# Two cached attention blocks on one core: the maximum over partitions moved from GpSimd to TensorE and VectorE, and the identity made without the library's select

## The chip, the cores and the metric

The kernel runs on one core of a Trainium2 chip. The time is the device time in microseconds of one execution, the median of several. In the profile PE is the matrix engine (TensorE), PEld its weight loads, DVE the vector engine, ACT the scalar engine, POOL GpSimd, SP the engine that issues most DMAs. Lines such as L338 are lines of the kernel file.

## The reference

Two blocks A and B of one decoding step each, side by side in the output. Both have 4 batches, 32 query heads, 8 key/value heads, head size 128, a cache of 8192 tokens; B looks only at the last 2048.

```python
q = (x @ wq).reshape(B, 1, 32, 128).transpose(0, 2, 1, 3)
k, v = repeat(k_cache, 4, axis=1), repeat(v_cache, 4, axis=1)   # B: last 2048 tokens
scores = einsum("bhqd,bhkd->bhqk", q, k) * 128 ** -0.5
o = einsum("bhqk,bhkd->bhqd", softmax(scores), v)
out = o.transpose(0, 2, 1, 3).reshape(B, 1, 4096) @ wo          # A and B concatenated
```

All inputs are bf16. The caches that are read, with the weights, are 184.6 MB.

## The kernel before

The work is cut into 20 units: four of block B (one batch with all 8 heads each), then sixteen of block A (one batch and two heads each). A unit has 4 MB of K and 4 MB of V, loaded into two slots each (`kv_load`). The 128 partitions of a slot hold different tokens, so a softmax runs over 128 partitions and 128 places in each. For block A the rows of 32 KB go to the partitions in the order 32 x 4, so that a partition's head follows from its number modulo 4; the masks `MASKA` and `MASKB` put -1e30 on the scores of the head that a partition does not hold.

Per unit `u`, in PE's order: K is transposed on PE in 16 groups of four f32 transposes (`pe_T`, L283) and copied out of PSUM by DVE and ACT in turn (L299); the scores are 16 groups of matmuls three groups behind (`pe_S`, L322), the first half into bank `SA[u % 2]`, the second into `SB`; near the end come the sums of the exponentials of the unit before (`pe_SM`, L350, into the other `SA`); and, after the last scores, the 128 matmuls of the unit before with its V (`pe_PV`, L338), in eight chunks of 16.

Meanwhile the maximum of unit `u` is taken: DVE reduces the two halves along the free dimension (`dve_max`, L420), adds the mask (`dve_addmask`, `M1m`), GpSimd reduces over the partitions and puts the result on all of them (`pool_ar1`, L441, `MB`), DVE takes the mask off (`dve_submask`, `MBm`), subtracts from both halves of the scores (`dve_sub`, L458), and ACT makes the exponentials (`act_exp`, L469). DVE takes the sum of the exponentials of the unit before (`dve_sum`, L476) between the masked maximum and `dve_submask`, and after the subtractions normalises the unit before (`add_norm`), whose end is `otr`.

Every two units (a turn of a hardware loop on PE; `turn`) one piece of the output projection runs beside the rest (`pe_job_OT`, `pe_job_OL`, `pe_job_OPJ`) and is added to `oacc` by DVE (L404, `ocp`).

Order comes from the order of each engine's list (`plan`) and from semaphores. SP issues the loads in one list: both Wq, K of units 0 and 1, then K(u), V(u-1) for each u, a piece of Wo for every second unit. V(u) waits for `otr(u-2)`, K(u) of block A for `otr(u-3)` (early ones for the transposes of u-2), the pieces of Wo for `ocp`; an entry that waits holds all behind it. V of the last unit comes in three chunks (`VL`), the last piece of Wo in eight (`WL`).

At the start GpSimd fills the buffers (`pool_setup0`, `pset`), makes the bf16 and f32 identities `ident` and `identf` by `affine_select` (`pool_setup1`, `setup`), the permutation `permE`, and from `EO`, which DVE reduces out of `ident`, the masks. The queries are made on PE (`pe_job_xT`, `pe_job_QP`, `pe_job_perm`), first for B, then for A; Wq lies in the V slots until then, so V(0) waits for B's queries. GpSimd copies each unit's queries to `RQc` (`pool_rq`).

The tail, after the loop: half of the last value product (chunks 0 to 3, with the first part of V), `pe_SM` of the last unit, `pe_seed` (L679: `oacc` put into two PSUM banks by f32 matmuls), the other four chunks, `add_norm`, 16 matmuls with the last piece of Wo (L700) on top of the seed, two copies and two stores.

Of the kernel before, what the change touches and what calls it, by code (L numbers as in the profile page):

```python
# [14 lines left out]
def bass_concat_heads__gqa_block_cached__sliding_block_cached__decode_kernel(  # L15
# [12 lines left out]
):  # L28
    ReduceOp = bass.bass_isa.ReduceOp

# [8 lines left out]
    NSEG = 4  # L39
# [33 lines left out]
    with ExitStack() as es:  # L73
# [8 lines left out]
        def sm(name):  # L82
# [16 lines left out]
        M1m = sb("M1m", [128, NSEG * C], F32)  # L99
        MB = sb("MB", [128, NSEG * C], F32)  # L100
        MBm = sb("MBm", [128, NSEG * C], F32)
# [11 lines left out]
        OTp = sb("OTp", [128, C, Bn], BF16)  # L113
        ORx = sb("ORx", [C * Bn, C, C, 128 // C], BF16)
        MSK = sb("MSK", [C * Bn, C], BF16)
        SEL = sb("SEL", [C * Bn, Bn], BF16)
        EO = [sb("EO%d" % P, [128, 2], F32) for P in range(2)]
        OL = sb("OL", [128, C, Bn], BF16)
# [9 lines left out]
                 "out0", "out1", "out2", "Tq", "Td", "Ta", "S", "PV", "Ed", "Ea", "Eq", "vs", "sub", "exp", "otr", "otp",  # L128
                 "ocp", "Ef", "fin0", "fin1", "ar1", "SM", "msk", "pset", "setup", "pm0", "pm1", "oc", "ocB", "mkb", "perm", "rq"]
        sems = {n: sm("s_" + n) for n in names}  # L130
# [103 lines left out]
        def pe_job_perm(P):  # L234
            idx = perm_idx[P] = new_job("perm", "act")
            bk = kbank(idx)

            def fn(pe):
                ins = None
                for e in range(2):  # L240
                    ins = pe.matmul(out=bk[:, e * Bn * HQ:(e + 1) * Bn * HQ],
                                    lhsT=permE[:, e, :, :].rearrange("p t i -> p (t i)"),
                                    rhs=QT[:, P, :, :].rearrange("p b h -> p (b h)"), start=True, stop=True)
                return ins
            op("pe", fn, waits=[("E", qp_idx[(P, NQP - 1)]), ("perm",), bankfree(idx)], inc=("T", idx))

            def efn(act):
                ins = None
                for tl in range(2):
                    ins = act.activation(  # L250
                        out=RQ[P][64 * tl:64 * tl + 64, :, :, :, C * tl:C * tl + C].rearrange("p b g e c -> p e (b g) c"),
                        in_=bk[64 * tl:64 * tl + 64, 0:2 * Bn * HQ].rearrange("p (e s c) -> p e s c", e=2, c=C), func=ACTF.Copy)
                return ins
            add(dict(eng="act", fn=efn, waits=[("T", idx)], inc=("E", idx)))

# [47 lines left out]
        def pool_rq(u):  # L303
            un = units[u]
            w = [("E", perm_idx[un["P"]])]
            if un["P"] == 1:
                src = RQ[1][:, un["b"], :, :, :]
            else:
                src = RQ[0][:, un["b"], un["gp"]:un["gp"] + 1, :, :].broadcast_to([128, NSEG, 2, 2 * C])
            return dict(eng="pool", fn=lambda pool: pool.tensor_copy(out=RQc[:, u % 2, :, :, :], in_=src), waits=w, inc=("rq", u))  # L310
# [16 lines left out]
        def pe_PV(u, c, bank=None, waits=()):  # L327
# [3 lines left out]
            def fn(pe):  # L331
# [8 lines left out]
                return ins  # L340
            op("pe", fn, waits=waits, inc=("PV", u * NC + c))

# [93 lines left out]

        def pool_ar1(u):
            n = ncol(u)

            def fn(pool):  # L440
                return pool.partition_all_reduce(MB[:, 0:n], M1m[:, 0:n], channels=128, reduce_op=ReduceOp.max)  # L441
            return dict(eng="pool", fn=fn, waits=[("pm", u, 0)], inc=("ar1", u))

        def dve_submask(u):
            n, P = ncol(u), units[u]["P"]

            def fn(dve):
                return dve.tensor_tensor(out=MBm[:, 0:n], in0=MB[:, 0:n], in1=MASK[P][:, 0:n], op=AluOpType.subtract)
            return dict(eng="dve", fn=fn, waits=[("ar1", u)], inc=("pm", u, 1))
# [71 lines left out]

        def pool_setup0(pool):
            pool.memset(dummy[:, :], 0.0)
            pool.memset(onesf[:, :], 1.0)
            pool.memset(onesb[:, :], 1.0)
            pool.memset(RQ[0][:, :, :, :, :], 0.0)
            pool.memset(RQ[1][:, :, :, :, :], 0.0)
            pool.memset(OT_sb[:, :, :, :, :], 0.0)
            pool.memset(oacc[:, :], 0.0)
            pool.memset(PT[:, :, :], 0.0)  # L530
            return pool.memset(Wo_sb[:, :, :], 0.0)
        op("pool", pool_setup0, inc=("pset",))

        def pool_setup1(pool):
            ins = pool.affine_select(out=ident[:, :], in_=onesb[:, :], pattern=[[1, 128]],
                                     compare_op=AluOpType.is_equal, fill=0.0, base=0, channel_multiplier=-1)
            ins = pool.affine_select(out=identf[:, :], in_=onesf[:, :], pattern=[[1, 128]],  # L537
                                     compare_op=AluOpType.is_equal, fill=0.0, base=0, channel_multiplier=-1)
            return ins
        op("pool", pool_setup1, waits=[("pset",)], inc=("setup",))  # L540

# [7 lines left out]
        def dve_msk(dve):  # L549
            idv = ident[0:NR, 0:NR].rearrange("p (h b) -> p h b", h=C)  # L550
            dve.tensor_reduce(out=EO[1][:, :], in_=ident[:, :].rearrange("p (i s) -> p s i", s=2), axis=AX.X, op=AluOpType.max)
            dve.tensor_reduce(out=EO[0][:, :], in_=ident[:, :].rearrange("p (i s m) -> p s i m", s=2, m=2), axis=AX.XY, op=AluOpType.max)
            dve.tensor_reduce(out=MSK[:, :], in_=idv, axis=AX.X, op=AluOpType.max)
            return dve.tensor_reduce(out=SEL[:, :], in_=idv.rearrange("p h b -> p b h"), axis=AX.X, op=AluOpType.max)
        op("dve", dve_msk, waits=[("setup",)], inc=("msk",))
        def pool_mask2(pool):
            for P, g in ((0, 1), (1, NSEG)):
                ins = pool.tensor_scalar(out=MASK[P][:, :].rearrange("p (g s h) -> p g s h", g=g, s=2),
                                         in0=EO[P][:, :].rearrange("p (g s h) -> p g s h", g=1, h=1).broadcast_to([128, g, 2, REP]),
                                         scalar1=-1.0, scalar2=BIG, op0=AluOpType.add, op1=AluOpType.mult)  # L560
            return ins
        op("pool", pool_mask2, waits=[("msk",)], inc=("mkb",))

        def dma(dst, src):
# [10 lines left out]
        for P in (1, 0):  # L575
# [3 lines left out]
            pe_job_perm(P)  # L579
        op("pe", None, waits=[("E", perm_idx[0]), ("setup",), ("msk",)])  # L580
        op("dve", None, waits=[("msk",)])
        add(pool_rq(0))
# [13 lines left out]
        while pc < NC:  # L596
            TOK.append(("PV", pc))
            pc += 1
        assert pc == NC
        AFTER = {("S", 2): ("OT",), ("S", 5): ("OL",)}  # L600

        for u in range(NU):
# [8 lines left out]
            for tok in TOK:  # L611
# [11 lines left out]
                elif tok[0] == "SM":  # L623
                    pe_SM(u - 1)
                else:
                    pe_PV(u - 1, tok[1], waits=[("V", u - 1) if u >= 1 else None] if tok[1] == 0 else [])
# [6 lines left out]
            for k in range(0, NJ, 2):  # L633
# [3 lines left out]
                for d in extra.get(k, []):  # L637
                    add(d)
            add(dve_max(u, 1))
            if units[u]["P"] == 0:  # L640
                add(dve_maxc(u))
            add(dve_addmask(u))
            if u >= 1:
                add(dve_sum(u - 1))
                add(dve_rcp(u - 1))
            add(dve_submask(u))
            add(dve_sub(u, 0))
# [18 lines left out]
            if u + 1 < NU:  # L666
                add(pool_rq(u + 1))
            add(pool_ar1(u))
            if u >= 1 and units[u - 1]["P"] == 0:
# [12 lines left out]
        add(dve_rcp(L))  # L682
        VCH = [4, 3, 1]
        vch_of = [i for i, n in enumerate(VCH) for _ in range(n)]
        for c in range(NC):
# [3 lines left out]
            if c == 4:  # L689
                pe_SM(L)  # L690
                op("pe", pe_seed, waits=[("ocp", NTURN - 1)])
            pe_PV(L, c, bank=KTB[0], waits=w)
# [15 lines left out]
        def kv_load(kind, u):  # L708
# [21 lines left out]
            if kind == "V" and u == L:  # L730
                c0 = 0
                for i, n in enumerate(VCH):
                    t0, t1 = c0 * TC, (c0 + n) * TC
                    src = bass.AP(tensor=base.tensor, offset=base.offset + t0 * DH, ap=[[NT * DH, 32], [32 * NT * DH, 4], [1, (t1 - t0) * DH]])
                    op("sp", dma(buf[:, slot, t0:t1, :].rearrange("p t d -> p (t d)"), src), waits=w, inc=("VL", i))
                    c0 += n
                return
            src = bass.AP(tensor=base.tensor, offset=base.offset, ap=[[NT * DH, 32], [32 * NT * DH, 4], [1, NT * DH]])
            sem = sem_of((kind, u))
            bump = 16 * (NPART[kind] - 1)  # L740
            op("sp", lambda sp: sp.sem_inc(sem, bump), waits=w, bump=(sem, bump, None))
            if kind == "K" and u == L:
                for h in range(2):
                    t0 = h * NTH
                    src = bass.AP(tensor=base.tensor, offset=base.offset + t0 * DH, ap=[[NT * DH, 32], [32 * NT * DH, 4], [1, NTH * DH]])
                    op("sp", dma(buf[:, slot, t0:t0 + NTH, :].rearrange("p t d -> p (t d)"), src), inc=(kind, u, 0) if h == 0 else ("KH", u))
# [189 lines left out]
```

## Time and profile before

| what | us |
|---|---|
| median of 5 runs | 439.43 (439.05 to 439.77) |
| the profiled execution, its own time | 439.61 |
| its span, first to last instruction | 437.6 |
| PE busy | 364.3 (83%) |
| DVE busy | 209.9 (48%) |
| ACT busy | 194.9 (45%) |
| POOL busy | 27.6 (6%) |
| POOL partition_all_reduce (L441), 20 times | 7.7 |
| first PE instruction (L201) | 20.61 |
| first K transpose (L283) | 34.00 |
| HBM read | 184.56 MB, 422 GB/s over the span |

How to read a profile line: start and length in microseconds, engine, line, operation, what it writes `<-` what it reads with partitions x elements, how many; in square brackets the idle time of the engine before it and what ended it. In the lines of the stage view the columns are the window, its length, the busy time of PE, PEld, DVE, ACT and POOL with the number of instructions, the granted clock of PE as a share of full speed, the busy share of the DMA engines, and GB/s. In the page's slices each digit is the busy share of a fortieth of the span in tenths. A PE that is busy is not a PE at its peak, since matmuls are pipelined.

### The profile page before, as it was taken

What the parts mean: (1) busy time and instruction counts of PE and PEld (TensorE: products, weight loads), DVE (VectorE), ACT (ScalarE), POOL (GpSimd) and SP (SyncE); (2) the same over time, 40 slices, a digit from 0 to 9 for tenths busy, and PEclk for the clock granted to TensorE, in tenths of its full rate; (3) what the DMA queues carried; (4) which work ended last, traced back from release to release, by engine and by line L of the source; (5) the groups of instructions that cost most, each with busy time, mean ns of one, the idle gap of its engine ahead of it and who ended that gap; (6) DMA issues with size and microseconds to landing.
All of it is one profiled execution on the core that took longest, in us unless ns stands there. A gap on an engine that the chain in (4) does not pass through costs nothing.

```text
span 437.6 us, 15525 instructions
## 1 busy us (share of the span) xinstructions
PE 364.3 (83%) x7174; PEld 337.3 (77%) x7184; DVE 209.9 (48%) x406; ACT 194.9 (45%) x249; POOL 27.6 (6%) x88
## 2 busy tenths in 40 slices
PE   0068998998998959896989598969878895989996
PEld 0068897997996959795979588868868795979975
DVE  0004555664564634463456247525644563456651
ACT  1024474473663625271635254434535361537540
POOL 6100000000000000000000000000100000000000
PEclk9999999999999997999999899989998999799999
DMA  8999999999999999999999999999999999999996
GB/s 336 433 428 412 427 415 428 420 443 407 449 431 434 422 435 431 434 425 434 431 431 428 431 431 428 435 429 431 419 443 431 431 429 431 431 431 419 437 421 237
DMA packets 10996, 184.73 MB, mean 422 GB/s; under 512 B 1236, under 2 KB 2280, under 8 KB 2408
## 3 DMA queue, kind: packets, MB, share of 16 engines
q1 hardware_dynamic: 10960, 184.56, 99.0%
q8 instruction: 8, 0.13, 0.1%
q10 hardware_dynamic: 24, 0.01, 0.0%
q14 instruction: 4, 0.03, 0.0%
HBM read 184.56 MB, written 0.01 MB: 422 GB/s over the span
## 4 chain that ended last, share of the span: by engine, by line
PE 54%; DMA 41%; issue 2%; DVE 1%; SPq 1%; ACT 1%
DMA K_sb<-in_A_k_cache_dram 29%; PE KT L283 26%; PE OT L338 11%; DMA K_sb<-in_B_k_cache_dram 7%; PE SB L322 5%; PE SA L322 4%; DMA V_sb<-in_A_v_cache_dram 4%; PE KT L396 4%; PE SA L350 1%; PE KT L338 1%; SPq L566 1%; DVE oacc L404 1%; PE KT L263 1%; ACT KT_sb L299 1%; DVE OS L501 0%
## 5 line engine op out<-in xcount | busy, mean ns | idle before, releaser
L283 PE MATMUL KT<-identf,K_sb 128*128 128x128 f32 x1280 | 206.8, 295 | 44.6 <-DMA K_sb<-in_A_k_cache_dram 32.3
L299 ACT ACTIVATE KT_sb<-KT 128x1024 bf16<-128x1024 bf16 (+1 forms) x192 | 165.0, 881 | 120.0 <-PE KT L283 120.0
L283 PEld LDWEIGHTS KT<-identf,K_sb 128*128 128x128 f32 x1280 | 146.8, 149 | 49.8 <-DMA K_sb<-in_A_k_cache_dram 33.2
L299 DVE COPY KT_sb<-KT 128x512 int32<-128x512 int32 x160 | 110.4, 690 | 131.9 <-PE KT L283 130.5
L338 PE MATMUL OT<-PT,V_sb 128*128 128x64 bf16 x2560 | 78.1, 193 | 1.0 <-issue 0.6
L338 PEld LDWEIGHTS OT<-PT,V_sb 128*128 128x128 bf16 x2560 | 75.9, 98 | 1.2 <-issue 0.7
L469 ACT ACTIVATE PT<-Dt 128x512 bf16<-128x512 f32 x40 | 24.6, 630 | 84.0 <-DVE Dt L458 84.0
L322 PEld LDWEIGHTS SA<-RQc,KT_sb 128*128 128x128 bf16 x1280 | 57.0, 98 | 2.3
L322 PEld LDWEIGHTS SB<-RQc,KT_sb 128*128 128x128 bf16 x1280 | 51.1, 97 | 7.9 <-issue 4.4
L322 PE MATMUL SA<-RQc,KT_sb 128*128 128x16 bf16 x1280 | 56.4, 170 | 0.0
L322 PE MATMUL SB<-RQc,KT_sb 128*128 128x16 bf16 x1280 | 52.9, 170 | 0.0
L420 DVE TENSOR_REDUCE M<-SB 128x8 f32<-128x512 f32 (+1 forms) x20 | 13.8, 692 | 50.1 <-PE SB L322 50.1
L441 POOL PARTITION_ALL_REDUCE MB<-M1m x20 | 7.7, 385 | 334.3 <-DVE M1m L434 334.3
L396 PE MATMUL KT<-Wo_sb,OL 128*4 128x512 bf16 x80 | 18.9, 379 | 0.0
L201 PE MATMUL KT<-ident,x_sb 4*128 4x4 bf16 x8 | 0.6, 170 | 20.6 <-POOL identf L537 20.6
L201 PEld LDWEIGHTS KT<-ident,x_sb 4*128 4x128 bf16 x8 | 0.4, 114 | 20.8 <-issue 20.8
L476 DVE TENSOR_REDUCE LB<-SA 128x8 f32<-128x512 f32 (+1 forms) x20 | 13.7, 684 | 2.8 <-PE SA L350 2.8
L458 DVE TENSOR_TENSOR Dt<-SA,MBm 128x512 f32<-128x512 f32 x20 | 13.8, 691 | 0.7
L367 DVE TENSOR_TENSOR ORx<-KT,MSK 32x1024 bf16<-32x1024 bf16 x10 | 12.1, 1212 | 3.5 <-PE KT L362 3.5
L458 DVE TENSOR_TENSOR Dt<-SB,MBm 128x512 f32<-128x512 f32 x20 | 13.6, 681 | 0.0
L420 DVE TENSOR_REDUCE M<-SA 128x8 f32<-128x512 f32 (+1 forms) x20 | 13.6, 681 | 0.0
L350 PE MATMUL SA<-PT,onesb 128*128 128x128 bf16 x168 | 12.7, 218 | 0.0
(69 smaller groups left out, 118.1 us busy)
## 6 DMA issues: line engine op xcount, KB each, us to landing
K_sb<-in_A_k_cache_dram SPq DMA_DIRECT2D x15, 4096.0 KB, 23.1
V_sb<-in_A_v_cache_dram SPq DMA_DIRECT2D x15, 4096.0 KB, 30.2
K_sb<-in_B_k_cache_dram SPq DMA_DIRECT2D x8, 2048.0 KB, 23.8
V_sb<-in_B_v_cache_dram SPq DMA_DIRECT2D x16, 1024.0 KB, 18.7
V_sb<-in_B_wq_dram SPq DMA_DIRECT2D x1, 4096.0 KB, 12.3
V_sb<-in_A_wq_dram SPq DMA_DIRECT2D x1, 4096.0 KB, 21.5
Wo_sb<-in_B_wo_dram SPq DMA_DIRECT2D x4, 1024.0 KB, 12.0
K_sb<-in_A_k_cache_dram SPq DMA_DIRECT2D x2, 2048.0 KB, 17.5
```

The lines of the kernel that those rows point to most:

```text
L283: ins = pe.transpose(out=bkf[:, pi * 128:(pi + 1) * 128], in_=K_sbf[:, slot, t0:t0 + 2, :].rearrange("p t d -> p (t d)"), identity=identf[ ...
L299: ins = e.tensor_copy(out=d, in_=r) if eng == "dve" else e.activation(out=d, in_=r, func=ACTF.Copy)
L322: ins = pe.matmul(out=stb[:, t % NTH * C:(t % NTH + 2) * C], lhsT=ktv[:, pi, :, e], rhs=RQc[:, u % 2, t // TS, e, :], start=(e == 0), stop ...
L338: ins = pe.matmul(out=otb[:, s * NW:s * NW + w], lhsT=V_sb[:, slot, t, :], rhs=PT[:, slot, t * C:t * C + w], start=(j == 0), stop=(j == n ...
L350: ins = pe.matmul(out=SA[u % 2][:, s * NM:(s + 1) * NM], lhsT=onesb[:, :], rhs=PT[:, u % 2, c0:c0 + NM], start=(i == 0), stop=(i == n - 1))
L367: return dve.tensor_tensor(out=ORx[:, :, :, :], in0=bk[0:NR, 0:128].rearrange("p (i o r) -> p r o i", o=1, r=C).broadcast_to([NR, C, C, 12 ...
L396: ins = pe.matmul(out=bk[0:Bn, 0:D], lhsT=OL[:, i, :], rhs=Wo_sb[:, i, :], start=(i == 0), stop=(i == C - 1))
L420: return dve.tensor_reduce(out=M1[:, h * n:(h + 1) * n].rearrange("p (s h) -> p s h", h=C), in_=bank[:, :].rearrange("p (s j h) -> p s h j ...
L441: return pool.partition_all_reduce(MB[:, 0:n], M1m[:, 0:n], channels=128, reduce_op=ReduceOp.max)
L458: return dve.tensor_tensor(out=Dt[:, h * NTH * C:(h + 1) * NTH * C].rearrange("p (s j h) -> p s j h", s=Sh, h=C), in0=bank[:, :].rearrange ...
L469: return act.activation(out=PT[:, u % 2, a:b], in_=Dt[:, a:b], func=ACTF.Exp, scale=scale)
L476: return dve.tensor_reduce(out=LB[:, 0:n].rearrange("p (s h) -> p s h", h=C), in_=SA[u % 2][:, 0:NSEG * NM].rearrange("p (s j h) -> p s h ...
```

## The change

- **Maximum over partitions.** PE transposes the masked maxima `M1m` into a free stretch of the `SA` bank of the unit before (`pe_MT`), DVE reduces each row (`dve_mx`), PE multiplies the broadcast column with the identity, which puts the maxima on all 128 partitions (`pe_MB`), and `dve_submask` reads them from PSUM. `pe_MT` stands after two chunks of the value product, `pe_MB` after four. `dve_sum` goes ahead of the last `dve_max`, so that the bank is free.
- **Identity.** DVE makes 1 to 32 along the free dimension by a scan over ones and transposes them in 32 x 32 blocks; GpSimd compares the two on the four diagonal blocks. `ident` is a copy of `identf`.
- **Order of the setup.** The large memsets come last on GpSimd (`pset`), and ACT's copies of the queries, PE and DVE wait for them.
- **Row order.** Block A's rows are loaded in plain order, so `MASKA` is four memsets.
- **Queries.** `pool_rq` waits for a new semaphore (`rqf`, raised by the first value chunk) where the all-reduce had kept it in step.
- **Tail.** `pe_seed` stands ahead of the last value product, no longer between its halves.

```diff
+        def pe_MT(u):
+            op("pe", lambda pe: pe.transpose(out=mtx(u), in_=M1m[:, :], identity=identf[:, :]), waits=[("pm", u, 0)], inc=("mt", u))
-        def pool_ar1(u):
-                return pool.partition_all_reduce(MB[:, 0:n], M1m[:, 0:n], channels=128, reduce_op=ReduceOp.max)
+        def dve_mx(u):
+            return dict(eng="dve", fn=lambda dve: dve.tensor_reduce(out=MX[0:n, :], in_=mtx(u)[0:n, :], axis=AX.X, op=AluOpType.max),
+                        waits=[("mt", u)], inc=("mx", u))
+        def pe_MB(u):
+            op("pe", lambda pe: pe.matmul(out=mbx(u), lhsT=MX[:, 0:1].broadcast_to([NX, 128]), rhs=identf[0:NX, 0:NX], start=True, stop=True), waits=[("mx", u)], inc=("ar1", u))
...
-            pool.memset(Wo_sb[:, :, :], 0.0)
-            ins = pool.affine_select(out=ident[:, :], in_=onesb[:, :], pattern=[[1, 128]],
+        op("dve", lambda dve: dve.tensor_tensor_scan(out=JC[:, :], data0=ONE[:, :], data1=ONE[:, :], initial=0.0, op0=AluOpType.mult,
+                                                     op1=AluOpType.add), waits=[("pl", 0)], inc=("jj", 0))
+        op("dve", lambda dve: dve.transpose(out=JR[:, :], in_=JC[:, :]), waits=[("jj", 0)], inc=("jj", 1))
+                ins = pool.tensor_scalar(out=identf[r, r], in0=JC[r, :], scalar1=JR[r, 0:1], scalar2=None, op0=AluOpType.is_equal)
...
+            if pc == 2:
+                TOK.append(("MT",))
+            if pc == 4:
+                TOK.append(("MB",))
...
+            if u >= 1:
+                add(dve_sum(u - 1))
             add(dve_max(u, 1))
...
-            if u >= 1:
-                add(dve_sum(u - 1))
+            add(dve_mx(u))
             add(dve_submask(u))
...
-            add(pool_ar1(u))
...
+        op("pe", pe_seed, waits=[("ocp", NTURN - 1)])
...
             if c == 4:
                 pe_SM(L)
-                op("pe", pe_seed, waits=[("ocp", NTURN - 1)])
...
-            src = bass.AP(tensor=base.tensor, offset=base.offset, ap=[[NT * DH, 32], [32 * NT * DH, 4], [1, NT * DH]])
+            src = bass.AP(tensor=base.tensor, offset=base.offset, ap=[[NT * DH, 128], [1, NT * DH]])
```

## The prediction

> **What bounds the kernel now.** I read the page's slices and queues first, then the DMA issues, then the timeline at three places: a unit's end, a wait for K, and the tail.
>
> ```profile
> PE   0068998998998959896989598969878895989996
> ...
> DMA  8999999999999999999999999999999999999996
> ...
> q1 hardware_dynamic: 10960, 184.56, 99.0%
> ...
> K_sb<-in_A_k_cache_dram SPq DMA_DIRECT2D x15, 4096.0 KB, 23.1
> V_sb<-in_A_v_cache_dram SPq DMA_DIRECT2D x15, 4096.0 KB, 30.2
> ...
> V_sb<-in_B_wq_dram SPq DMA_DIRECT2D x1, 4096.0 KB, 12.3
> ```
>
> The 16 DMA engines are busy 99.0% of the span, at 9 tenths or more from the second slice to the last but one; TensorE is not. The chain of waits gives PE 54% and DMA 41%, which misleads: it follows PE wherever PE issued something, while the DMA line shows that no transfer was ever missing. The issues say how far ahead the queue runs. A 4 MB load needs about 9.7 us of the engines (4.19 MB at the 431 GB/s of the late slices), yet K lands 23.1 us and V 30.2 us after its issue: 13 and 20 us of older transfers stood before it. Summing issued less moved bytes at each issue, I find the smallest lead at three issues: 7.5 us at 54.6, 7.9 us at 123.8, 7.2 us at 391.9. In the packet records the first payload starts at 1.83 us and the last Wl_sb packet ends at 434.49 us. The span is then 1.8 us of start, 432.7 us of saturated transfers and 3.1 us of tail. An edit counts only if it changes the transfer rate, makes the queue run dry, or lengthens the tail.
>
> A unit's end (unit 18), where the maximum is taken:
>
> ```profile
> 404.98 3.79 PEld L338 LDWEIGHTS OT<-PT,V_sb 128*128 128x128 bf16 x128
> 405.00 3.89 PE L338 MATMUL OT<-PT,V_sb 128*128 128x64 bf16 x128
> 405.19 0.69 DVE L420 TENSOR_REDUCE M<-SB 128x8 f32<-128x512 f32 x1 [1.87 <-PE SB L322]
> ...
> 406.11 0.17 DVE L434 TENSOR_TENSOR M1m<-M1c,MASKA 128x8 f32<-128x8 f32 x1
> ...
> 406.38 0.37 POOL L441 PARTITION_ALL_REDUCE MB<-M1m  x1 [13.97 <-DVE M1m L434]
> ...
> 407.04 0.11 DVE L448 TENSOR_TENSOR MBm<-MB,MASKA 128x8 f32<-128x8 f32 x1
> ```
>
> The value matmuls run from 405.00 without a break while DVE and GpSimd find the maximum beside them: GpSimd's step costs PE nothing.
>
> The last wait for K, with the busy times and granted clock (PEclk, the column before the DMA share) just before and in it:
>
> ```profile
> 371.24 3.67 PE L283 MATMUL KT<-identf,K_sb 128*128 128x128 f32 x16 [4.97 <-DMA K_sb<-in_A_k_cache_dram]
> ```
>
> ```profile
> 366.50:370.20 3.70, 0.00 (x0) 0.00 (x0) 0.17 (x1) 0.00 (x1) 0.42 (x2) 1.00 1.01 434
> 370.50:377.00 6.50, 5.76 (x41) 5.58 (x42) 2.08 (x3) 2.05 (x2) 0.00 (x0) 0.50 1.01 434
> ```
>
> PE waits 4.97 us for K of unit 17, then runs at half clock to about 377; 16 transposes take 3.67 us where they take 1.78 at full clock. That wait is also PE's reserve: being late is forgiven there, once in two units.
>
> The tail:
>
> ```profile
> 426.63 0.67 DVE L404 TENSOR_TENSOR oacc<-KT,oacc 4x512 f32<-4x512 f32 x1
> ...
> 427.65 1.98 PE L338 MATMUL KT<-PT,V_sb 128*128 128x64 bf16 x64 [1.36 <-DMA V_sb<-in_A_v_cache_dram]
> ...
> 430.02 0.59 PE L679 MATMUL SA<-oacc,identf 4*4 4x256 f32 x2
> ...
> 430.98 1.92 PEld L338 LDWEIGHTS KT<-PT,V_sb 128*128 128x128 bf16 x64 [0.44 <-DMA V_sb<-in_A_v_cache_dram]
> ...
> 434.98 0.08 PEld L700 LDWEIGHTS KT<-Wl_sb,OT_sb 128*4 128x4 bf16 x1 [0.22 <-DMA Wl_sb<-in_A_wo_dram]
> ```
>
> Each step of it waits for a landing: the first half of the last value product (427.65), the second (430.98), the last piece of Wo (434.98).
>
> **The change part by part.**
>
> *Setup.* Before, PE's first instruction waits until 20.61 for the identity, behind 7.3 us of GpSimd memsets and an idle of 11.81 us. The memsets now come after the identity, about 1.9 us of small GpSimd work ahead of it. The built program still has one library reload, in front of the first tensor_scalar; only the one for the all-reduce is gone. So the identity comes at about 3 us if that reload costs nothing (the library may be resident), or at 1.9 + 11.8 + some 0.9 = 14.6 us if it costs what the idle shows. With the later one, masks and memsets end at about 24 us, the second half of the queries at about 30 us. The first K transpose waits for K, landed at 34.00, either way; if that cover were gone, the 6 to 17 us would count. On SP the first V load waits for the first queries (24.82 now, 17 to 19 then) with 17 us of transfers still queued, so its earlier issue moves nothing. Price: 0.
>
> *Order of the rows in the A loads* (134 of 184.6 MB): 128 rows of 32 KB in plain order instead of 32 x 4. Plain order is in the trace: the two Wq loads have it, with 1.213 us for nearly every 32 KB packet, and the first lands in 12.3 us with the start-up in it. The A loads take 1.217 on the mean. That is no gain of the plain order, since B's 32 x 4 loads also sit at their floor (0.611 us for 16 KB) before the compute starts and at 0.614 once it runs. I take 0. Bounds: -0.9 us if the plain order holds 1.213 (3,840 packets / 16 engines x 3.7 ns); and to be fair the same +0.9 the other way.
>
> *The maximum.* Per unit PE gets a transpose after 32 of the 128 value matmuls and a broadcast after 64, each with a wait in PE's queue; behind them stand the other value matmuls and the next unit's transposes. M1m is ready 1.28 us after the first value matmul (405.00 to 406.28); PE is there after 0.94 (32/128 of 3.75). It stands 0.34 + 0.05 (an ACT end at 40.78 let PE go at 40.83) = 0.39 us. The transpose costs 0.11 (16 of L283 in 1.78) to 0.30 (its whole 295 ns); the broadcast, 32 f32 columns, 0.05 (256 columns of L679 follow at 0.43) to 0.30. The new DVE reduction, about 0.29 (EO's 128x128 reduce at L551), plus 0.30 of transpose and two hand-overs of 0.05 make 0.69, inside the next 0.94 of value matmuls. The sum of the exponentials moves ahead of the last maximum, into DVE's idle 1.87 us. So d, what each unit adds to PE, is 0.39 + 0.11 + 0.05 plus some 0.07 for the weight loads = 0.62, with bounds 0.5 and 1.0; a gain is excluded, since PE only gets work and waits. GpSimd loses 20 x 0.385 us that nobody waited for.
>
> The Trainium skill speaks against this edit: "GPSIMD Engine Reference", section 4.1 Engine selection, gives a reduction along partitions to GpSimd. The trace agrees in kind (0.385 us per call off PE's path); by the page the edit loses, by the rows it loses d per unit, of which the K waits take most.
>
> In the loop d costs nothing. Seven units to 141 us pile up 7 x 0.62 = 4.3 us against leads of at least 7.5; from then on each two units add 1.24 to a 4.2 to 5.3 us wait. If the leads were gone, 20 x 0.62 = 12.4 us would show.
>
> *The tail.* After the last forgiven wait (371.24) units 17, 18 and 19 each add d, and the seed moves ahead of the last value product, where it waits for oacc. The chain: value matmuls of unit 18 at 421.78 + 2d (but not before V's landing, 422.38), their sum on DVE 3.94 + d later, oacc done 0.98 later, seed 0.05 + 2 x 0.43, the half product and sums 2.37, the rest 2.36 + 15 x 0.1085 to the last Wo matmul. That is 433.97 + 3d, against 435.09 now: 3d - 1.12 = +0.74 us with d = 0.62; 0.4 and 1.9 at the bounds. This keeps the half clock up to 377. But the wait of 4.97 shrinks by 2d to 3.7 us. All six long waits (4.24 to 5.26) were followed by half clock, none of the 1.4 us ones at the loop's end; 3.7 is nearer the first, so some slowing stays, but four of the six cost 1.0 to 1.2 us less (16 transposes in 3.07 to 3.57, unit 18.4 to 18.6 us instead of 19.65). With that or with no slowing unit 18 starts early enough that V's landing at 422.38 rules, and the end is at d - 0.52 = +0.1 us (0 to 0.5). I take +0.1.
>
> "TensorE: Matmul & The Clock Gate", Part 1, of the skill says the clock halves after an idle window of about 3.4 us. With it a 3.7 us wait would mostly stay at full clock: +0.1 us again, against +0.74 with the slowing exactly as in this trace.
>
> Sum: 439.61 (span 437.6 and 2.0 around it) + 0 + 0 + 0.1 = 439.7 for an execution like the profiled one, which is 0.18 above the median of 439.43; so 439.6.
>
> **The rivals.**
>
> *Slower: PE reaches the tail late.* For it: no slack is left at 430.98, where the seed's end and V's landing meet, and three d arrive there with one more wait on DVE. With the long half clock it passes 0.88 us (0.2%, about what can be told from no change) from d = 0.67; at d = 0.9 it is 3 x 0.9 - 1.12 = 1.6 us, 441.1. Against: it needs the longest of the six slowings again. Chance 0.30, with the +0.9 of the row order in it.
>
> *Faster: packets at their floor.* The A loads at 1.213 would pull every landing forward: 439.5 - 0.9 = 438.6. Against: the excess came with the compute in both row orders. Chance 0.15, with a luckier spread of the engines (2.5 us between first and last at every late landing).
>
> *The change doesn't do what it says:* the remaining reload keeps the identity at 14.6 us. The time is the forecast's, 439.6; it is counted there.
>
> **How the numbers follow.** Forecast 0.55: 439.6, its own range 439.0 to 440.3. Slower 0.30, faster 0.15. For 8 in 10 I reach to 438.6 below and to 441.3 above (d = 1.0 with long half clock: 439.43 + 1.9).
>
> **What would show it.** Right: DMA digits still 9 throughout, last Wl_sb packet near 434.5, PE standing 0.3 to 0.5 us before the new transpose and hardly before the broadcast, K waits near 3.7 us, oacc done and seed between 428 and 430. Wrong: 32 KB packets off 1.217 us, a DMA slice below 9, more than 1 us added per unit, or K no longer what the first transpose waits for.

## The result, and the profile after

| | before | after |
|---|---|---|
| median | 439.23 us (438.95 to 439.91, 49 runs) | 440.46 us (439.35 to 443.58, 27 runs) |
| ratio | | 1.0039 (95%: 1.0029 to 1.0049) |
| profiled execution, its time | 439.61 us | 440.33 us |
| its span | 437.6 us | 438.5 us |
| last packet of `Wl_sb` | 434.49 us | 434.22 us |
| last matmul with Wo starts | 435.09 us | 436.06 us |

The change makes the kernel slower, by 0.39% in the ratio, which here is that of the means; the medians differ by 1.23 us, 0.28%. The time lies inside the stated 438.6 to 441.3 us, but outside the 439.0 to 440.3 that the likeliest case had for itself: PE reaches the tail late, as in the rival of that name. The runs before lie within 1 us of each other; the runs after lie in three clusters, about 439.5, 440.4 and 442 to 443.6 us. The profiled one is of the middle cluster, where the median is.

The page of the kernel after: DMA digits by slices, the loads' queue, and the chain of waits.

```profile
DMA  8999999999999999999999999999999999999995
...
q1 hardware_dynamic: 10960, 184.56, 98.8%
...
PE 60%; DMA 30%; DVE 5%; issue 3%; SPq 1%; ACT 0%
...
K_sb<-in_A_k_cache_dram SPq DMA_DIRECT2D x15, 4096.0 KB, 20.3
```

The transfers are as they were: nines throughout, 98.8% of a span that is 0.9 us longer, K still landing 20.3 us after its issue (23.1 before). The last packet even lands 0.27 us earlier. All of the loss lies behind it: 435.09 to 436.06, with the end of the kernel after it as before. In the chain the DMA's share fell from 41% to 30% and PE's rose from 54% to 60%, and here that does mean something: waits that forgave PE's lateness have shrunk.

The setup, from the timeline after (start, length):

```profile
1.85 1.65 POOL L558 TENSOR_SCALAR identf<-JC,JR 32x32 f32<-32x32 f32 x4 [0.19 <-POOL MASKA L551]
...
4.00 0.26 PE L203 MATMUL KT<-ident,x_sb 4*128 4x4 bf16 x4 [4.00 <-POOL ident L561]
```

GpSimd goes into the comparison 0.19 us after its last memset, where it stood for 11.81 us before, so the remaining reload costs nothing that shows; PE begins at 4.00, not 20.61, then waits for Wq until 13.24. The first K transpose starts at 34.24, after a wait of 6.00 us for K. As predicted, 16 us of an earlier start are worth nothing.

A unit's end (unit 19's maximum, the value product of unit 18), and the sum on DVE that follows it, after and then before:

```profile
422.46 1.09 PE L340 MATMUL OT<-PT,V_sb 128*128 128x64 bf16 x32
...
423.57 0.17 DVE L436 TENSOR_TENSOR M1m<-M1c,MASKA 128x8 f32<-128x8 f32 x1
...
423.79 0.28 PE L448 MATMUL SA<-identf,M1m 128*32 128x128 f32 x1 [0.24 <-DVE M1m L436]
...
423.91 1.10 PE L340 MATMUL OT<-PT,V_sb 128*128 128x64 bf16 x32
...
424.94 0.40 PE L456 MATMUL SA<-identf,MX 32*128 32x32 f32 x2
...
425.27 0.90 PE L340 MATMUL OT<-PT,V_sb 128*128 128x64 bf16 x25
...
427.35 0.19 DVE L515 TENSOR_REDUCE OS<-OT 128x8 f32<-128x32 f32 x1 [0.48 <-PE OT L340]
```

```profile
426.32 0.19 DVE L501 TENSOR_REDUCE OS<-OT 128x8 f32<-128x32 f32 x1 [1.05 <-PE OT L338]
```

Here the value matmuls, unbroken before, stop twice. The transpose could start 0.94 us after 422.46, at 423.40, and starts at 423.79 when `M1m` is there: 0.39 us of standing. It takes 0.12 (423.79 to 423.91). The broadcast takes 0.33 (424.94 to 425.27): the line says "x2", the 32 f32 columns are issued as two passes. From the start of the value matmuls to the sum on DVE it was 3.94 us before (422.38 to 426.32) and is 4.89 now (422.46 to 427.35): d = 0.95 us per unit. The three parts make 0.84. Of the remaining 0.11 about 0.09 lies ahead of the broadcast: the 32 matmuls from 423.91 need 0.94 and would end at 424.85, and it starts at 424.94. Why, no line shows.

The last wait for K and the next loop end, from PE's timeline; the same loop end before; and the granted clock (the column before the DMA share) after that wait:

```profile
370.90 3.41 PE L285 MATMUL KT<-identf,K_sb 128*128 128x128 f32 x16 [2.48 <-DMA K_sb<-in_A_k_cache_dram]
...
391.94 2.10 PE L285 MATMUL KT<-identf,K_sb 128*128 128x128 f32 x16 [1.66 <-issue]
```

```profile
392.24 2.10 PE L283 MATMUL KT<-identf,K_sb 128*128 128x128 f32 x16 [1.35 <-issue]
```

```profile
370.50:374.00 3.50, 3.10 (x15) 3.10 (x16) 0.93 (x2) 1.02 (x1) 0.00 (x0) 0.51 1.02 440
374.00:378.00 4.00, 4.00 (x74) 3.93 (x73) 2.10 (x4) 3.00 (x3) 0.00 (x0) 1.00 0.95 410
```

The wait for K is 2.48 us (4.97 before), and the half clock after it lasts 3.4 us (6.8 before). The idle at the loop's end, put down to "issue", was 1.35 us before (1.35 to 1.44 over the turns) and is 1.66 now (1.66 to 1.74): two more semaphores that PE waits on, each of which the program lowers there.

The tail, from the timeline:

```profile
426.33 0.98 PE L340 MATMUL OT<-PT,V_sb 128*128 128x64 bf16 x28
...
427.66 0.67 DVE L406 TENSOR_TENSOR oacc<-KT,oacc 4x512 f32<-4x512 f32 x1
...
428.84 0.59 PE L715 MATMUL SA<-oacc,identf 4*4 4x256 f32 x2 [1.52 <-DVE oacc L406]
...
429.79 1.99 PE L340 MATMUL KT<-PT,V_sb 128*128 128x64 bf16 x64
...
434.43 0.27 PE L736 MATMUL KT<-Wl_sb,OT_sb 128*4 128x256 bf16 x1 [0.32 <-issue]
```

No step waits for a landing any more. From 428.84 to the end PE works without a gap but for the normalisation; its own chain sets the end.

The loss in the profiled execution's time, 0.72 us, is smaller than the 0.97 us of the tail: the span grew by 0.9 us, but the time around it fell from 2.0 to 1.8, so that 439.61 became 440.33.

### The profile page after: what moved, and what is told of

Read it like the earlier page. It is cut to its first block, busy times and chain, and to the rows that moved or that the text cites. A ratio compares the mean times of both kernels' runs of the same rounds, so it can differ in the third digit from the quotient of the medians.

```text
span 438.5 us, 15682 instructions
## 1 busy us (share of the span) xinstructions
PE 374.9 (85%) x7234; PEld 344.1 (78%) x7244; DVE 218.2 (50%) x427; ACT 194.8 (44%) x249; POOL 21.5 (5%) x76
## 3 DMA queue, kind: packets, MB, share of 16 engines
q1 hardware_dynamic: 10960, 184.56, 98.8%
## 4 chain that ended last, share of the span: by engine, by line
PE 60%; DMA 30%; DVE 5%; issue 3%; SPq 1%; ACT 0%
PE KT L285 29%; DMA K_sb<-in_A_k_cache_dram 23%; PE OT L340 10%; DMA K_sb<-in_B_k_cache_dram 7%; PE SB L324 5%; PE SA L324 5%; PE KT L398 4%; DVE M L422 2%; PE SA L352 2%; PE SA L456 1%; PE SA L448 1%; DVE oacc L406 1%; PE KT L340 1%; SPq L593 1%; PE KT L265 1%
## 5 line engine op out<-in xcount | busy, mean ns | idle before, releaser
L285 PE MATMUL KT<-identf,K_sb 128*128 128x128 f32 x1280 | 203.6, 292 | 34.8 <-issue 15.1
L285 PEld LDWEIGHTS KT<-identf,K_sb 128*128 128x128 f32 x1280 | 143.9, 147 | 39.9 <-issue 16.2
L340 PE MATMUL OT<-PT,V_sb 128*128 128x64 bf16 x2560 | 84.8, 193 | 0.2 <-issue 0.2
L340 PEld LDWEIGHTS OT<-PT,V_sb 128*128 128x128 bf16 x2560 | 80.0, 98 | 1.4 <-issue 0.3
L226 PE MATMUL KT<-xT,V_sb 128*128 128x4 bf16 x256 | 7.1, 166 | 15.2 <-DMA V_sb<-in_B_wq_dram 9.0
L226 PEld LDWEIGHTS KT<-xT,V_sb 128*128 128x128 bf16 x256 | 7.0, 104 | 15.4 <-DMA V_sb<-in_B_wq_dram 9.1
L524 POOL COPY OT_sb<-ON 128x8 bf16<-128x8 bf16 x15 | 3.0, 201 | 293.1 <-DVE ON L518 293.1
## 6 DMA issues: line engine op xcount, KB each, us to landing
K_sb<-in_A_k_cache_dram SPq DMA_DIRECT2D x15, 4096.0 KB, 20.3
```

Of the source, the lines that this page charges most:

```text
L226: ins = pe.matmul(out=bk[:, hl * Bn:(hl + 1) * Bn], lhsT=wv[:, c, hq * DH:(hq + 1) * DH], rhs=xT[:, P, c, :], start=(c == 0), stop=(c == D ...
L285: ins = pe.transpose(out=bkf[:, pi * 128:(pi + 1) * 128], in_=K_sbf[:, slot, t0:t0 + 2, :].rearrange("p t d -> p (t d)"), identity=identf[ ...
L340: ins = pe.matmul(out=otb[:, s * NW:s * NW + w], lhsT=V_sb[:, slot, t, :], rhs=PT[:, slot, t * C:t * C + w], start=(j == 0), stop=(j == n ...
```

## The experiments

Theory going in: the setup and the row order are worth nothing, and the loss is d, left over behind the last wait for K, with the loop end's 0.3 us on top. Rivals: the seed's new place, or a clock that halves in the tail. Each kernel was timed over five rounds against the kernel before on the same chip; ratios are to that, with 95% intervals, and are not simply those of the medians. Medians of before in these calls were 439.06 to 439.21.

### Each part alone

**The seed back between the halves of the last value product**, all else as after:

```diff
-        op("pe", pe_seed, waits=[("ocp", NTURN - 1)])
...
                 pe_SM(L)
+                op("pe", pe_seed, waits=[("ocp", NTURN - 1)])
```

> The changed kernel with the seed back between the halves of the last value product. Theory (PE is late by about 0.95 us per unit for the maximum, and the tail became PE's own chain): the two seed matmuls cost their 0.9 us in either place, so about 440.4 us as in the changed kernel, within 0.4. Rival (the seed's new wait for oacc is the cost): back to the kernel before, 439.2 to 439.6.

440.54 us (439.58 to 440.69), 1.0025 (1.0016 to 1.0034). Two runs at 439.6, nine at 440.4 to 440.7, none at 442 or more, as expected. So the seed's place doesn't make the median; it does go with the slowest cluster. The profiled run (440.47) has 3.4 us of half clock after the last wait for K, as the kernel after.

**The maximum on GpSimd again**, setup, rows and seed as after:

```diff
+            add(pool_ar1(u))
-            add(dve_mx(u))
-            if pc == 2:
-                TOK.append(("MT",))
-            if pc == 4:
-                TOK.append(("MB",))
```

> The changed kernel with the maximum over partitions on GpSimd again; setup, row order and place of the seed as changed. Theory (the maximum on PE is the cost): 439.0 to 439.5 us, a value product of 3.9 us without a break, K waits of 4 to 5 us again, a loop end of 1.4 us. Rivals (row order, setup or seed): about 440.4 stays.

439.51 us (439.26 to 440.70), 1.0013 (1.0004 to 1.0022). The loop end is back at 1.38 us and the waits for K at up to 5.3. Most of the loss is gone, so it came with the maximum; this kernel keeps the moved sum and the new semaphore of the queries, so it isn't theirs. Three of eleven runs are still at 440.35 to 440.70.

**The maximum on PE alone**, put into the kernel before:

```diff
-            add(pool_ar1(u))
+            add(dve_mx(u))
+            if pc == 2:
+                TOK.append(("MT",))
+            if pc == 4:
+                TOK.append(("MB",))
```

> The kernel before with only the maximum over partitions moved to PE and DVE (with the order of the sum and the semaphore that it needs). Theory: all of the loss, 440.0 to 441.0 us in the median, with the same spread of more than 2 us between runs as the changed kernel; a unit's value product about 0.95 us longer, loop end 1.7 us for 1.4. Rivals (row order, setup, seed): 439.2.

441.14 us (439.37 to 441.27, 5 runs), 1.0039 (1.0026 to 1.0053): the whole loss of the change, without the setup, the rows or the seed, and 0.14 us more than was expected at most. The loop end is 1.66 us. Its profiled run is the quick one, 439.37. In it the last wait for K is 1.52 us, and there is no half clock after it:

```profile
370.00:374.00 4.00, 3.40 (x49) 3.37 (x50) 2.08 (x3) 1.99 (x3) 0.00 (x0) 1.00 1.01 434
374.00:378.00 4.00, 4.00 (x76) 3.93 (x74) 2.05 (x4) 3.02 (x3) 0.00 (x0) 1.00 0.91 393
```

So PE reaches the value product of unit 18 early, waits 0.84 us for V there (start at 421.74), and its lateness is forgiven once more. The mean clock of this run is 0.984, that of its three slowest 0.981, but the run at 440.50 has 0.977. In the kernel after it is 0.984 in four of the five quickest runs, and in the middle cluster 0.981 in eight runs and 0.984 in five: a hint of the same parting and no more, as no quick run of the kernel after left a profile. What the three slowest here hold, at 441.1 to 441.3 where the kernel after has no run, is open too.

**The seed moved alone**, in the kernel before:

```diff
+        op("pe", pe_seed, waits=[("ocp", NTURN - 1)])
...
                 pe_SM(L)
-                op("pe", pe_seed, waits=[("ocp", NTURN - 1)])
```

> The kernel before with only the seed moved ahead of the last value product. Theory: PE is free at 427.65 and needs 0.9 + 2.4 us to the second half, which is where V's landing at 430.98 holds it anyway, so 439.2 us within 0.3. Rival (the seed's new place costs by itself): 440 or more.

439.94 us (439.06 to 440.34), 1.0012 (1.0003 to 1.0021): a miss by some 0.4 us at the median. Four runs lie at 439.06 to 439.37 and seven at 439.75 to 440.34. The profiled run (439.75) shows full clock in its tail, and its second half of the value product still waits 0.22 us for V, at 431.24: in that run the seed is off the path, as expected. The mean clock of the runs doesn't part the two groups. Moving the seed costs something by itself; by what, no profile here shows.

**Setup and rows alone** (maximum on GpSimd and seed back: the two edits above together):

> The changed kernel with the maximum on GpSimd again and the seed back between the halves: what is left of the change is the setup and the row order. Theory: neither is on the path that sets the end, 439.0 to 439.4 us, ratio 1.000 within 0.001, spread below 1 us. Rival (plain row order or the new setup costs or gains): 0.5 us or more from 439.2 on either side.

439.50 us (439.20 to 439.87), 1.0008 (0.9999 to 1.0017): not to be told from no change, though the median is 0.1 us above what was expected. The runs above 440.3 that the kernel with the seed ahead had are gone. In the packet records the 32 KB packets of the A loads take 1.217 us on the mean with plain rows here, 1.217 before.

GpSimd's way to the identity, with the maximum alone on PE (old setup, no all-reduce), and here (new setup, all-reduce kept):

```profile
8.20 0.29 POOL L546 TENSOR_SCALAR_AFFINE_SELECT ident<-onesb 128x128 bf16<-128x128 bf16 x1
```

```profile
13.76 1.66 POOL L567 TENSOR_SCALAR identf<-JC,JR 32x32 f32<-32x32 f32 x4 [12.10 <-issue]
```

The long idle ahead of the identity goes with the all-reduce and not with the select. With the all-reduce it is 11.81 us ahead of the select (before) and 12.10 and 12.44 us ahead of the comparison (here and in the kernel with the maximum on GpSimd again); without it the select follows the last memset at once, and PE begins at 8.89 with the old setup. PE begins at 15.91 here, so this run tests 4.7 us of an earlier start; that 16 us are worth nothing rests on the 6.00 us for which PE waits for K in the kernel after.

**The kernel after once more:**

> The changed kernel once more, beside its variants. Its 27 runs lie in three groups, near 439.5, 440.4 and 442 to 443.6 us, while the kernel before stays within 438.9 to 439.9. Theory (the last wait for K is followed by none, one or two half-clock windows of PE, and PE now sets the end): the same groups here, and the profile shows a half clock of 6.8 us after 370 us if its time is above 442, 3.4 us if about 440.4, none if about 439.5. Rival (the slow group belongs to the seed's new place, as the variant with the seed put back had none of it in 11 runs): a time above 442 with half clock in the tail after 427 us.

440.37 us (439.39 to 443.54), 1.0034 (1.0015 to 1.0054), with the three clusters again: four runs at 439.4 to 439.6, five at 440.2 to 440.6, three at 442.0 to 443.5. They belong to the kernel, not to a chip. The profiled run (440.58) has 3.4 us of half clock after the last wait for K and none in the tail, as was expected of a run near 440.4.

### Making d smaller

**Transpose after three chunks, broadcast after five:**

```diff
-            if pc == 2:
+            if pc == 3:
                 TOK.append(("MT",))
-            if pc == 4:
+            if pc == 5:
                 TOK.append(("MB",))
```

> The changed kernel with the transpose of the maxima after three chunks of the value product and the broadcast after five (two and four in the changed kernel). Theory: PE's stand before the transpose (0.39 us) goes, each unit is about 0.4 us shorter, three units 1.2 us, so 439.3 to 439.8 us. Rival (what counts is the later exponentials, not PE's stand): same or slower than 440.4.

**The broadcast in bf16** (the scores' maxima rounded to bf16, so the softmax is shifted by the rounded value):

```diff
-        MX = sb("MX", [NSEG * C, 1], F32)
+        MX = sb("MX", [NSEG * C, 1], BF16)
-rhs=identf[0:NX, 0:NX]
+rhs=ident[0:NX, 0:NX]
```

> The changed kernel with the reduced maximum in bf16 and the bf16 identity, so that the broadcast is a bf16 matmul; the maximum that is subtracted is rounded, alike on all partitions. Theory: the broadcast costs PE 0.33 us in f32, in two passes, and about 0.1 in bf16, so three units are 0.7 us shorter: 439.6 to 440.0 us. Rival (the hand-over costs, not the matmul): 440.4.

**Both:**

> Both: transpose after three chunks, broadcast after five, broadcast in bf16 (the maximum that is subtracted is rounded, alike on all partitions). Theory: a unit's value product about 4.2 us for 4.9, the last wait for K near 4 us, the end set by the transfers again: 439.1 to 439.5 us with a spread below 1 us. Rival: the loss stays, 440 or more.

441.07 us (439.63 to 442.82), 1.0043 (1.0029 to 1.0056); 441.33 (439.00 to 442.75), 1.0043 (1.0024 to 1.0062); 440.69 (439.09 to 440.89), 1.0031 (1.0021 to 1.0041). All three missed: PE's path per unit did get shorter (the standing is gone with the later chunks, and the bf16 broadcast is one pass of 0.11 us; d is 0.54, 0.73 and 0.33 us), and the median didn't fall. The profiled run of the first (442.22 us, 2.5 of them outside the span) shows a reason. The tail from its timeline, and a stage of it beside the same stage of the kernel after, which has the same order of work:

```profile
428.51 0.59 PE L715 MATMUL SA<-oacc,identf 4*4 4x256 f32 x2 [1.55 <-DVE oacc L406]
...
429.46 2.52 PE L340 MATMUL KT<-PT,V_sb 128*128 128x64 bf16 x64
...
435.60 0.27 PE L736 MATMUL KT<-Wl_sb,OT_sb 128*4 128x256 bf16 x1 [0.32 <-issue]
```

```profile
430.50:433.80 3.30, 3.30 (x65) 3.30 (x62) 0.87 (x2) 0.00 (x0) 0.00 (x0) 0.51 0.85 281
```

```profile
430.50:433.80 3.30, 3.30 (x113) 3.30 (x110) 0.90 (x2) 0.00 (x0) 0.00 (x0) 1.00 0.92 301
```

The clock is halved from 430.5 on: 65 matmuls in the 3.3 us instead of 113, and 429.46 to 435.60 = 6.14 us for what takes 4.64 in the kernel after (429.79 to 434.43). PE had stood 1.55 us ahead of the seed, and the seed is 0.95 us of matmuls of four rows. The profiled run with the bf16 broadcast, at its median, has the same from 430.1 on (clock 0.50). The profiled run of both (439.09, the quickest) stands for 1.55 us ahead of the same seed and keeps full clock, so the stand and the seed don't always bring it. And with a smaller d the wait for K can grow (4.76 us in the first), and the half clock around it is 6.8 us again: from K to the loop's end PE takes 21.46 us (370.93 to 392.39) where it takes 21.04 in the kernel after with 0.41 more of d, so about 0.8 us are given back.

### All together

**Later chunks, bf16 broadcast, and the seed back between the halves:**

> The changed kernel with transpose after three chunks, broadcast after five and in bf16 (the maximum that is subtracted is rounded, alike on all partitions), and the seed back between the halves of the last value product. Theory as it stands now (two costs: PE arrives late by the work of three units, and the seed's new place puts its small f32 matmuls next to the idle loop end, so that PE's clock is halved in the tail in some runs): both are gone, 439.0 to 439.4 us, no run above 440, no half clock after 427 us. Rival (the half clock in the tail comes with PE being late, not with the seed's place): a group near 440.7 as without the seed put back.

439.61 us (439.39 to 439.77), 1.0012 (1.0003 to 1.0021): 0.2 us above what was expected at most, but one cluster. Both edits without the seed stood 1.5 us above the kernel before at the median, this one stands 0.55 above it: some 1.0 us by the seed's place alone. PE's timeline:

```profile
424.64 0.18 PE L456 MATMUL SA<-ident,MX 32*128 32x32 bf16 x1
424.75 1.57 PE L340 MATMUL OT<-PT,V_sb 128*128 128x64 bf16 x48
427.99 1.98 PE L340 MATMUL KT<-PT,V_sb 128*128 128x64 bf16 x64 [1.66 <-ACT PT L483]
...
433.67 0.27 PE L736 MATMUL KT<-Wl_sb,OT_sb 128*4 128x256 bf16 x1 [0.32 <-issue]
```

No half clock is left behind 427 in this profile; d is 0.33; what remains is the loop end, 1.66 us here too (the wait at 427.99 is the exit of the loop, whatever the bracket names).

**The same with one semaphore less for each new wait**: PE's two new waits use the semaphore that DVE's copies raise already.

```diff
+            if t == "mx" or t == "pm" and key[2] == 0:
+                return sems["Ed"]
```

> The kernel with all three repairs, and the two new waits of PE (on the masked maxima and on the reduced maximum) counted on the semaphore by which DVE reports its copies to PE anyway. Theory: each semaphore that PE waits for in the loop has to be lowered at the loop's end, and the two new ones are the 0.3 us by which that end grew (1.66 for 1.38 us). The loop end goes back to 1.36 to 1.40 us and the time from 439.6 to 439.1 to 439.4. Rival (the loop end grew for its length in instructions or for fetching them): 1.66 and 439.6 stay.

439.39 us (439.00 to 439.68), 1.0003 (0.9994 to 1.0012), as expected. The loop end in PE's timeline:

```profile
391.09 2.10 PE L287 MATMUL KT<-identf,K_sb 128*128 128x128 f32 x16 [1.35 <-PEq L926]
```

```profile
427.60 1.98 PE L342 MATMUL KT<-PT,V_sb 128*128 128x64 bf16 x64 [1.33 <-ACT PT L485]
...
433.29 0.27 PE L738 MATMUL KT<-Wl_sb,OT_sb 128*4 128x256 bf16 x1 [0.32 <-issue]
```

1.35 us again, and the first matmul with Wo 0.38 us earlier than at 433.67: the two semaphores were the 0.3 us of each loop end. The idle shows it, not the time, as the intervals of the two kernels overlap.

**The improved maximum in the kernel before**, with its old setup, rows and seed:

> The kernel before with the maximum on PE and DVE, transpose after three chunks, broadcast after five and in bf16 (the maximum that is subtracted is rounded, alike on all partitions), both waits on the copies' semaphore; setup, row order and seed as before. Theory: the transfers set the end as in the kernel before, and the time outside the span is 0.3 us less without the all-reduce's library (1.70 for 2.00): 438.8 to 439.2 us, no run above 439.9. Rival (a value product cut in three still costs at the tail): 439.5 or more.

439.14 us (438.95 to 439.58), 0.9997 (0.9988 to 1.0006), as expected: the time of the kernel before, with no work of GpSimd in the maximum. Its time outside the span is 1.9 us, not the 1.7 seen with the maximum alone. Nothing tried beats the kernel before by more than the interval. In the kernel before the last Wo matmuls wait for their piece; in the profiled run here (439.46) they wait for none and go from 433.38 to 435.01, beside 433.34 to 435.09 before, so PE's chain is now about as long as the transfers.

## Why the prediction was right or wrong

*Right.* The transfers bound the kernel and weren't touched. The setup was worth 0, with the identity at 3.9 us where "about 3 us if that reload costs nothing" stood; the idle of 11.81 us, which the prediction's later case gave to the remaining reload, goes with the all-reduce. The row order was worth 0 (1.217 us packets in both). Standing before the transpose, 0.39 us, and the transpose, 0.12, were as worked out. In the loop d is absorbed by the waits for K, as said: 4.97 went to 2.48, by 2 x 0.95 and 0.3 of the loop end, with K landing 0.3 earlier. The half clock after it fell to the shorter length, as said, though at a wait well under the 3.7 us that was expected. That most of such a wait would pass at full clock, the other case of the prediction, did not hold: all five waits for K of 2.48 to 3.40 us in the kernel after were followed by 3.4 us of half clock.

*The step that failed*, though the time fell inside the range, is the sum for the tail, "the end is at d - 0.52 = +0.1 us". In the profiled run it is +0.97. Three terms were off:

- *d.* It is 0.95, not 0.62, near the upper bound of 1.0. The broadcast was put at 0.05 by the f32 matmuls of L679, whose 256 columns follow each other at 0.43; it costs 0.33, more than the 0.30 taken for its upper bound, as two passes. That is 0.28 of the difference; the stops took 0.11 where 0.07 stood for the weight loads. Together +0.33 for the one unit, 18, that the sum still counted.
- *PE late at V.* "V's landing at 422.38 rules" held for d = 0.62. With 0.95 and the loop end the value product starts at 422.46 with no wait. V's last packet is signalled at 422.01 in the packet records of the kernel after. So +0.08 against the row of before, and 0.4 us that the earlier landing could have given.
- *The loop end.* It was in no part of the sum. Two semaphores more make it 1.66 instead of 1.35 us, and its exit sets the start of the tail: the value product of unit 18 ends at 427.31, and PE goes on at 428.84, 0.51 us after `oacc` is done (428.33), where 0.05 was taken: +0.46. In the two kernels with the seed ahead but without the two semaphores the seed starts 0.20 and 0.23 us after `oacc`, so about 0.3 of it are the semaphores and the rest the exit as it was. The prediction had misread the row of before: it took the start at 427.65 for V's landing, as the bracket says; the loop's exit from 426.29 on, 1.36 us long, ends there too, and the packet records have V landed at 427.24.

0.10 + 0.33 + 0.08 + 0.46 = 0.97. PE did reach the tail late, as the rival has it, but not by the rival's sum: its formula, 3d - 1.12 with the long half clock, gives 1.7 at this d, and the half clock was the shorter one: from K to the loop's end PE took 21.0 us before (371.24 to 392.24) and 21.0 after (370.90 to 391.94), with 0.95 of d and 0.31 of loop end more in it, so 1.2 us less of slowing. K landed 0.3 earlier. The loop end gave 0.3 and 0.5 back. That leaves 1.0. So the time lies in the range by way of a rival whose own sum was off by 0.8 us: it had too much slowing and no loop end.

*Not foreseen* is the cluster at 442 to 443.6. With the seed ahead of the last value product the clock may halve in the tail, which takes 1.5 us more. This is shown in the profiles of two variants of the kernel after, and the cluster is absent from the five timed kernels that have the new maximum and the old seed's place. It is not shown in the kernel after itself, whose slowest runs left no profile; their spans are 440.3 to 441.2 us beside 438.4 to 439.0 in the middle cluster, and their mean clock, 0.973 to 0.977 beside 0.981 to 0.984, is about what one more stretch of 3.4 us at half clock makes (1.7 of 438 us, 0.004). What the seed's move costs in the kernel before without d, 0.4 us at the median, stays open.

The chances were wrong in their order: with d near its upper bound and no term for the loop, "slower" got 0.30. For the broadcast, the one operation that no row resembled, the forecast took the lower bound.

## What to carry to other kernels

When transfers set the end, an edit to a compute engine is priced only by what it adds after the last wait that forgives lateness; count there all that the edit brings, the semaphores at the loop's end too, and read the idle before an instruction by arithmetic, as the releaser named can be one that had come already. A new wait can ride on a semaphore that the same producer already raises, and a small matmul whose shape no row shows should be priced at its upper bound. An idle that goes away need not go by the edit that was meant to remove it: look for it in the variants that lack the edit. Here it also paid to keep thin matmuls away from the idle stretch ahead of the last big product.

## What the hardware showed beside that

- A 32-column f32 matmul against 32 rows is two passes and 0.33 us of PE's path; the same in bf16 is one pass and 0.11 us.
- Two further semaphores that PE waits on in the loop cost 0.3 us at every loop end (1.35 to 1.66 us, and back to 1.35 without them), so about 0.15 each if they are alike.
- The half clock came in pieces of 3.4 us, one or two of them. In the fourteen profiles, from 40 us on, every wait of PE for K of 3.1 us or more came with it and none below 2.19 us did; of the fifteen waits of 2.19 to 2.82 us nine did (2.19, 2.48 and 2.60, say) and six did not (2.28, 2.72 and 2.80, say).
- In the tail it came after only 1.55 us of idle with 0.95 us of four-row matmuls behind it, in two profiles; three others with 1.52 to 1.55 us of idle ahead of the same matmuls kept full clock.
- With the all-reduce in the kernel GpSimd stood idle for 11.8 to 12.4 us at the start, ahead of the select or of the comparison; without it, not at all.
- The time outside the span isn't constant: 2.0 us before, 1.8 after, 2.2 with the all-reduce and the new setup, 1.8 to 2.1 within the eleven runs of the kernel with one semaphore less, and up to 2.8 in the slowest runs.
